# Feed-forward quarters per step redistributed around the tail step of each head pair, input sums moved with them

## The chip, the cores and the metric

The kernel runs on one core of a Trainium2 chip. The core has five engines with in-order queues: TensorE (PE in the profile, with PEld for its weight loads), VectorE (DVE), ScalarE (ACT), GpSimd (POOL) and SyncE (SP, which issues nearly all transfers here), and 16 DMA engines. The metric is the device time of one execution in microseconds; smaller is better.

## The reference

```python
scores = scale * np.matmul(q, k.transpose(0, 1, 3, 2))        # q, k, v: (8, 8, 576, 64)
thresh = np.max(scores, axis=-1, keepdims=True) - tau
scores = np.where(scores >= thresh, scores, -1000000000.0)
attn = np.exp(scores - np.max(scores, axis=-1, keepdims=True))
attn = attn / (np.sum(attn, axis=-1, keepdims=True) + 1e-09)
x = np.matmul(attn, v)                                        # -> (8*576, 512)
h = x @ w_in                                                  # 512 -> 2048
g = np.where(h > 0.0, h, np.exp(np.minimum(h, 0.0)) - 1.0)
out = g @ w_out                                               # 2048 -> 512
```

Attention with a threshold under each row's maximum, for 8 sequences of 8 heads, and then a feed-forward block (FFN) with an ELU between its two products. All is float32.

## The kernel before, in words

**Attention.** Heads go in pairs: 32 pairs, four to a sequence. A pair has five steps: four blocks of 128 queries for both heads, and one tail step for the 64 queries left over of each head. From pair 9 (`JOINED`) the order in a pair is block 0, block 1, tail, block 2, block 3; the text calls these places 0 to 4, so the tail step is place 2. A step of two heads runs so: scores on TensorE (`scores`, L236), row maximum on VectorE (L276), bound on GpSimd (L280), exponential on ScalarE (L285, L287), threshold mask and row sum on VectorE (L296 to L303), division on GpSimd (L272). One step later VectorE turns the weights in squares of 32 (`turn_squares`, L380, L390), SyncE writes them out (L394, L406), and one step after that fetches them back turned (`fetch`, L414, L418). The value products of the pair before run inside the tail step, interleaved with the tail's scores (`tails_and_values`, L466, L471, L478); ScalarE copies their result out (`values_out`, L487, L492). Two PSUM buffers named `sc` (one per head) serve the scores, and in the tail step one of them holds the values instead.

**FFN.** Each product is done on halves with seven products in place of eight, so there are sums of inputs, of weights and of results. A group is 512 tokens of one sequence; group g has two rounds r. A round is four units of the first product (`first_product`, L1016), 28 quarters, and then a second product (`second_round`, L1171) of 14 products in two quarters each, 28 quarters again. A quarter is four matmuls as the profile counts them. Behind a unit, ScalarE copies partial results out (L1030, L1082, L1083), GpSimd adds (L1035), VectorE adds (L1038), and then the ELU runs: exponential on ScalarE (L1049, and minus one at L1054, or on GpSimd at L1063), minimum and maximum on VectorE (L1071). GpSimd then forms sums of the results for the second product (L1108). The second product's results are added up on VectorE (L1180, L1189, L1191) and GpSimd (L1184) and stored (L556). Sums of weights are kept in DRAM and reloaded (`sw` L871 for the first product, `t` L901 for the second). `sums_x` (L907 to L909) makes five sums of a group's inputs, two of them in place, on VectorE; they have to follow the last values of that sequence and precede most of the group's first quarters.

**Order.** From step 45 (`MIDDLE`, pair 9, place 0) to the end of attention the order is written by hand as an agenda with times: `on_pe(cost, f)` issues TensorE work and advances a planned clock, and `at(t, f)` puts the other engines' work at planned times. In each step the loop issues the fetch, `softmax(n)` (the attention step), then `ffn_quarters(QUARTERS[place])`, which takes that many quarters from a queue of first and second products in fixed order. `QUARTERS` sums to 28, so each pair takes one first or one second product: odd pairs the first, even pairs the second. `group(b - 1)` puts the next group's products on the queue at place 3 of the first pair of a sequence, where its input sums are issued as well. `exp` of a unit is put off to 4.4 us after the start of a step when it would fall in the step's early part, except for the last unit's first half; ELUs put off in this way run at the end of a later step (`run_elus`), or when the second product asks for them. After the loop, what is left on the queue is taken without attention beside it, and then the last two groups follow.

Of the kernel before, what the change touches and what calls it, by code (L numbers as in the profile page):

```python
# [19 lines left out]
def kernel(  # L20
# [24 lines left out]
    NPAIR = H // 2  # L45
# [329 lines left out]
    def turn_squares(pr, i):  # L375
        w = open_steps.pop((pr, i))["w"]
        x = late["x"].tile([P, NT, NCH, T], FP32, name="x", bufs=2)

        def turn_part(c0, src, nc_):
            nc.vector.transpose(x[:, :, c0 : c0 + nc_], src.rearrange("p (c g n) -> p g c n", c=nc_, n=T))  # L380

        if i < NC:
            turn_part(0, w[:, :MAIN], NC)
            turn_part(NC, w[:, MAIN : MAIN + P], 1)
            turn_part(NC + 1, w[:, MAIN + P :], NC)
        elif pr >= JOINED:
            turn_part(1, w[:, :MAIN], NC)
            tail = w[:, MAIN:S].rearrange("p (g n) -> p g n", n=T).unsqueeze(1).broadcast_to([P, 2, 2, T])
            for g in (0, 2):
                nc.vector.transpose(x[:, g : g + 2, :: NC + 1].rearrange("p g c n -> p c g n"), tail)  # L390
            there = turns[pr, i] = dram.tile([NT, T, NT, (NC + 1) * T], FP32, name="there")
            for p in range(NT):
                h = int(p < 2)
                nc.sync.dma_start(  # L394
                    there[:, :, (p + 2) % NT].rearrange("c k n -> k c n"),
                    x[p * T : (p + 1) * T, :, 1 - h : NC + 2 - h].rearrange("k c j n -> k c (j n)"),
                )
            return
        else:
            turn_part(0, w[:, :MAIN], NC)  # L400
            turn_part(NC + 1, w[:, :MAIN], NC)
            for h in range(2):
                nc.vector.transpose(x[:, 2 * h : 2 * h + 2, NC], w[:, MAIN:S].rearrange("p (g n) -> p g n", n=T))
        there = turns[pr, i] = dram.tile([NT, T, NT, NCH * T], FP32, name="there")
        for p in range(NT):
            nc.sync.dma_start(  # L406
                there[:, :, p].rearrange("c k n -> k c n"), x[p * T : (p + 1) * T].rearrange("k c j n -> k c (j n)")
            )

    def fetch(pr, i):  # L410
        back = turns.pop((pr, i)).rearrange("c k p n -> (c k) p n")
        wT, g0 = turned_tile(pr, i)
        if i < NC:
            nc.sync.dma_start(wT[:, g0 : g0 + NT].rearrange("p g c n -> p g (c n)"), back)  # L414
        elif pr >= JOINED:
            for h in range(2):
                g = h * (3 * NT - 2)
                nc.sync.dma_start(  # L418
                    wT[:, g : g + 2, h * NC : h * NC + NC + 1].rearrange("p g c n -> p g (c n)"),
                    back[:, 2 * h : 2 * h + 2],  # L420
                )
        else:
            nc.sync.dma_start(
                wT.rearrange("p (a b) c n -> p a b (c n)", b=2)[:, ::5],
                back.rearrange("k (a b) n -> k a b n", b=2),
            )
# [163 lines left out]
    JOINED = (2 * NPAIR + 1)  # L590
    steps = [(pr, i) for pr in range(NP) for i in ((0, 1, NC, 2, 3) if pr >= JOINED else range(NB))]
# [42 lines left out]
    with tc.manual_schedule():  # L634
# [20 lines left out]
        for n in range(per_seq):  # L655
            pr, i = steps[n]
            hs = heads_of(i)
            x = progress[1]
# [86 lines left out]
    with tc.manual_schedule():  # L745
# [3 lines left out]
        for n in range(per_seq, SWITCH):  # L749
            pr, i = step = steps[n]  # L750
# [152 lines left out]
    def sums_x(g, rooms):  # L903
        (b11, b12), (b21, b22) = ([xts[g][:, k : k + 2, t : t + CT] for t in (0, CT)] for k in (0, 2))
        xs = in_sums["x", g] = rooms
        tt = nc.vector.tensor_tensor
        return [lambda: tt(xs[0], b11, b22, ALU.add), lambda: tt(xs[1], b11, b12, ALU.add),  # L907
                lambda: tt(b12, b12, b22, ALU.subtract), lambda: tt(xs[2], b21, b22, ALU.add),
                lambda: tt(b21, b21, b11, ALU.subtract)]  # L909
# [6 lines left out]
    with tc.manual_schedule():  # L916
        after = []
        make_out(1), make_out(0)
        for n in range(SWITCH, MIDDLE):
            pr, i = steps[n]  # L920
# [15 lines left out]
            else:  # L936
                if n == MIDDLE - 2:
                    jobs = sums_x(1, [late["x"].tile([P, 2, CT], FP32, name=f"x{x}") for x in range(3)])
# [26 lines left out]
        agenda, clock, now, serial = [], [0.0], [0.0], [0]  # L965

        def at(t, f):
            serial[0] += 1
            heapq.heappush(agenda, (t, serial[0], f))
# [9 lines left out]
        def on_pe(cost, f):  # L979
            until(clock[0])  # L980
            f()
            clock[0] += cost
            return clock[0]
# [245 lines left out]
        def group(g):  # L1229
            for r in range(2):  # L1230
                for u in range(RU * r, RU * r + RU):
                    queue.append((first_product, (g, u)))
                queue.append((second_round, (g, r)))
# [3 lines left out]
        def ffn_quarters(n):  # L1237
            while n and (quarters or queue):
                if not quarters:
                    f, a = queue.popleft()  # L1240
                    running[0] = f
                    mine = f(*a)

                    if (f, a) == (second_round, (B, 1)):
                        mine = [mine[x] for x in (0, 2, 6, 1, 3, 4, 5)] + mine[7:]
                    quarters.extend(mine)
                p, posts = quarters.popleft()
                end = on_pe(QT, p)
                for lag, f in posts:
                    at(end + lag, f)  # L1250
                n -= 1
# [45 lines left out]
        def values_of(pr, i):  # L1297
            if i in (1, NB - 1) and pr < JOINED:
                loc = {}
                part = 0 if i == 1 else 1  # L1300
                end = on_pe(3.1 if part else 2.3, lambda: loc.update(out=values(pr, part)))
                at(end + 0.1, lambda: loc["out"]())
# [6 lines left out]
            for out_ in outs:  # L1309
                out_()  # L1310

        QUARTERS = (7, 6, 2, 7, 6)
        group(1)
        for n in range(MIDDLE, len(steps) + 3):
            pr, place = divmod(n, NB)
            if n <= len(steps) + 1:
                at(clock[0] + (3.4 if place == 2 else 1.5), lambda n=n: fetch(*steps[n - 2]))
            if 0 < n - MIDDLE < 4:
                x = n - MIDDLE - 1
                at(clock[0] + 5.0, lambda x=x: nc.sync.dma_start(wout_sums[0, x], out_sums[x].rearrange("p u n -> p (u n)")))  # L1320
            if n == MIDDLE + NB:
                ges.append((raw.tile([P, S // T, T], FP32, name="km").rearrange("p j d -> p (j d)")[:, : 2 * CT], lambda: None))
            if n == len(steps):
                at(clock[0] + 2.0, lambda: turn_squares(*steps[-1]))
            if n < len(steps):
                softmax(n)
            b = pr // NPAIR
            if n < len(steps) and pr % NPAIR == 0 and place == 3 and b > 1:
                xs = [late["x"].tile([P, 2, CT], FP32, name=f"x{x}") for x in range(3)]
                jobs = sums_x(b - 1, xs)  # L1330
                for x, f in enumerate(jobs):
                    at(clock[0] + 4.2 + 0.5 * x + (4.0 if x > 2 else 0), f)
                group(b - 1)
            if n == len(steps) + 2:
                on_pe(5.0, last_values)
            ffn_quarters(QUARTERS[place])
            values_of(*steps[n - 3])
        attending[0] = False
        xs = [late["x"].tile([P, 2, CT], FP32, name=f"x{x}") for x in range(3)]
# [43 lines left out]
        xs = [qkp.tile([P, S], FP32, name="qT") for _ in range(2)] + [qkp.tile([P, TAIL + S], FP32, name="kT")]  # L1383
        xs = [x[:, : 2 * CT].rearrange("p (k t) -> p k t", k=2) for x in xs]
# [47 lines left out]
```

## Time and profile before

| | us |
|---|---|
| median of 6 runs | 1429.79 |
| lowest and highest run | 1426.63, 1439.89 |
| profiled execution, its own time | 1435.87 |
| its span, first to last instruction | 1434.0 |
| TensorE busy in the span | 1356.0 |
| VectorE, GpSimd, ScalarE busy | 1064.8, 817.1, 640.2 |
| mean granted TensorE clock | 0.985 |

The profile's page gives each engine's busy time and its share of the span; the views by line give, for a group of instructions, busy time, mean duration and the idle time of the engine just ahead of them with what ended it. In a timeline a row is a run of like instructions: start and length in us, engine, line, operation, output and inputs, shape, count, and in brackets the idle time before it and who ended it. The loop that the change touches runs from about 310 to 1234 us of the span; before it the attention of the first sequences runs with the weights' conversion, and after it only FFN work is left.

### The profile page before, as it was taken

How to read it: one execution, taken by the hardware profiler on the slowest of the kernel's cores; microseconds unless marked ns; L12 is line 12 of the kernel's file. 1: busy time of each engine (PE TensorE's matmuls, PEld its weight loads, DVE VectorE, ACT ScalarE, POOL GpSimd, SP SyncE). 2: the span in 40 equal slices, each digit the busy share in tenths (PEclk: the TensorE clock that was granted, in tenths of full speed). 3: DMA queues.
4: the chain of work that ended last, by engine and by line, in shares of the span. 5: the costliest groups of instructions: out<-in, count | busy, mean ns of one | idle time of the engine just before them, and what ended most of it. 6: DMA issues, size and time to landing. Idle time of an engine off the chain costs nothing.

```text
span 1434.0 us, 22711 instructions
## 1 busy us (share of the span) xinstructions
PE 1356.0 (95%) x6980; PEld 1006.9 (70%) x6980; DVE 1064.8 (74%) x2325; ACT 640.2 (45%) x1418; POOL 817.1 (57%) x1274
## 2 busy tenths in 40 slices
PE   9989999999999999998999999989999998999998
PEld 7656646556767677676767776767767676888887
DVE  6879995988778778887788778877787775546433
ACT  5776764235453536353444535353535443223311
POOL 4656774787466555656475647555564645425423
PEclk9998999999999999999999999999999999999999
DMA  5345433889878878686969787887879674421311
GB/s 111 73 108 144 132 101 77 252 245 256 222 199 225 219 186 239 174 241 174 239 168 272 171 230 200 237 215 178 235 175 252 165 224 124 137 66 46 117 55 30
DMA packets 322599, 247.80 MB, mean 173 GB/s; under 512 B 208688, under 2 KB 284464, under 8 KB 322480
## 3 DMA queue, kind: packets, MB, share of 16 engines
q1 hardware_dynamic: 320112, 246.07, 64.7%
q8 instruction: 56, 0.92, 0.3%
q10 hardware_dynamic: 2368, 0.30, 0.2%
q14 instruction: 63, 0.52, 0.1%
HBM read 161.81 MB, written 84.48 MB: 172 GB/s over the span
## 4 chain that ended last, share of the span: by engine, by line
PE 63%; DVE 14%; DMA 8%; POOL 6%; issue 4%; ACT 3%; SPq 2%; DVEq 0%; ACTq 0%; POOLq 0%
PE f L1171 20%; PE f L1016 16%; PE sc L236 8%; PE pv L478 6%; DVE mx L276 3%; PE rt L306 3%; DMA wTb<-there 3%; DMA there<-x 3%; DVE x L380 2%; PE f L527 2%; PE pv L440 2%; POOL s L1108 2%; PE f L567 2%; DVE w L296 2%; DVE g L1071 2%
## 5 line engine op out<-in xcount | busy, mean ns | idle before, releaser
L272 POOL TENSOR_SCALAR w<-w,rs 128x576 f32<-128x576 f32 x288 | 241.0, 841 | 152.4 <-DVE rs L303 135.5
L276 DVE TENSOR_REDUCE mx<-sc 128x1 f32<-128x576 f32 x270 | 193.0, 752 | 107.9 <-PE sc L236 82.6
L296 DVE SCALAR_TENSOR_TENSOR w<-sc,th,e 128x576 f32<-128x576 f32 x270 | 215.2, 813 | 34.1 <-ACT e L287 13.9
L287 ACT ACTIVATE e<-sc,nb,keep 128x576 f32<-128x576 f32 x270 | 223.2, 832 | 9.1 <-POOL nb L673 0.7
L285 ACT ACTIVATE nb<-mx,nkeep 128x1 f32<-128x1 f32 x254 | 74.7, 294 | 306.2 <-DVE mx L276 306.1
L236 PE MATMUL sc<-kT,qT 64*128 64x288 f32 x1024 | 175.7, 431 | 9.1 <-DVE w L296 7.8
L380 DVE STREAM_TRANSPOSE x<-w 128x512 f32<-128x512 f32 (+1 forms) x327 | 167.5, 560 | 0.0
L280 POOL TENSOR_SCALAR th<-mx,ntau 128x1 f32<-128x1 f32 x270 | 82.4, 306 | 146.7 <-DVE mx L276 145.4
L1171 PE MATMUL f<-w_out_sb,g 128*128 128x256 f32 x448 | 117.1, 396 | 40.6 <-DVE g L1071 40.6
L236 PEld LDWEIGHTS sc<-kT,qT 64*128 64x128 f32 x1024 | 99.2, 187 | 69.9 <-issue 48.8
L1016 PE MATMUL f<-xt,sw 128*128 128x256 f32 x512 | 130.1, 389 | 0.3 <-DVE g L1038 0.3
L1171 PEld LDWEIGHTS f<-w_out_sb,g 128*128 128x128 f32 x448 | 83.9, 194 | 65.1 <-DVE g L1071 50.6
L1016 PE MATMUL f<-xt,w_in_sb 128*128 128x256 f32 x512 | 121.1, 379 | 0.5 <-ACT w L1030 0.5
L1171 PE MATMUL f<-t,s 128*128 128x256 f32 x448 | 113.5, 387 | 1.4 <-DVE s L1108 0.7
L1016 PEld LDWEIGHTS f<-xt,sw 128*128 128x128 f32 x512 | 93.2, 190 | 29.9 <-issue 17.7
L1016 PE MATMUL f<-x,w_in_sb 128*128 128x256 f32 x448 | 109.0, 382 | 0.0
L1171 PE MATMUL f<-w_out_sb,s 128*128 128x256 f32 x448 | 108.8, 382 | 0.0
L1016 PEld LDWEIGHTS f<-xt,w_in_sb 128*128 128x128 f32 x512 | 97.2, 190 | 14.0 <-ACT w L1030 0.9
L1171 PEld LDWEIGHTS f<-t,s 128*128 128x128 f32 x448 | 82.1, 190 | 26.6 <-issue 8.2
L1016 PEld LDWEIGHTS f<-x,w_in_sb 128*128 128x128 f32 x448 | 84.1, 190 | 16.8 <-issue 5.4
L1035 POOL TENSOR_TENSOR u<-u,w 128x256 f32<-128x256 f32 x64 | 46.9, 733 | 85.1 <-ACT u L1030 85.1
L1171 PEld LDWEIGHTS f<-w_out_sb,s 128*128 128x128 f32 x448 | 84.2, 190 | 15.2 <-issue 4.2
(176 smaller groups left out, 2475.2 us busy)
## 6 DMA issues: line engine op xcount, KB each, us to landing
there<-x SPq DMA_DIRECT2D x408, 144.0 KB, 2.8
wTb<-there SPq DMA_DIRECT2D x52, 576.0 KB, 4.8
wTa<-there SPq DMA_DIRECT2D x50, 576.0 KB, 4.6
sw<-win_sums SPq DMA_DIRECT2D x62, 384.0 KB, 4.3
t<-wout_sums SPq DMA_DIRECT2D x45, 512.0 KB, 5.1
qm<-in_q_dram SPq DMA_DIRECT2D x128, 72.0 KB, 4.8
vm<-in_v_dram SPq DMA_DIRECT2D x64, 128.0 KB, 4.1
wst<-in_moe_w_in_dram SPq DMA_DIRECT2D x16, 512.0 KB, 4.6
```

Of the source, the lines that this page charges most:

```text
L236: nc.tensor.matmul(scs[h][:, a, :HALF], qs[r], kT[r, k0 : k0 + HALF], start=True, stop=True)
L272: nc.gpsimd.tensor_scalar(wv, wv, st["rs"][:, h : h + 1], 1.0, ALU.mult, ALU.mult)
L276: nc.vector.tensor_reduce(st["mx"][:, h : h + 1], st[h][:, :, :HALF], axis=AX.XY, op=ALU.max)
L280: nc.gpsimd.tensor_scalar(st["th"][:, h : h + 1], st["mx"][:, h : h + 1], 1.0, ntau, ALU.mult, ALU.add)
L285: nc.scalar.mul(st["nb"][:, h : h + 1], st["mx"][:, h : h + 1], nkeep)
L287: nc.scalar.activation(e, st[h][:, :, :HALF], AF.Exp, bias=st["nb"][:, h : h + 1], scale=keep)
L296: nc.vector.scalar_tensor_tensor(wv, sc[:, :, :HALF], st["th"][:, h : h + 1], e, ALU.is_ge, ALU.mult, accum_out=st["sm"][:, h : h + 1])
L380: nc.vector.transpose(x[:, :, c0 : c0 + nc_], src.rearrange("p (c g n) -> p g c n", c=nc_, n=T))
L478: nc.tensor.matmul(pv[h * D : (h + 1) * D, part, g0 * T : g1 * T], vm[:, h, c], parts[part][:, g0:g1, h * (NC + 1) + c], start=False, stop ...
L1016: nc.tensor.matmul(loc["banks"][place], left[:, j], right[:, j], start=(begins and j == 0), stop=(j == 1), skip_group_check=True)
L1035: nc.gpsimd.tensor_tensor(loc[name], x(), loc[other], op)
L1171: nc.tensor.matmul(place(m), lhs, rhs, start=(begins and v == 0), stop=(v == RU - 1), skip_group_check=True)
```

## The change

The five quotas of a pair keep their sum of 28 but are 7, 7, 2, 6, 6 instead of 7, 6, 2, 7, 6. Pair 9 has quotas of its own, 14, 14, 0, 6, 6, so that the queue runs 12 quarters ahead of the pairs from then on: a pair's quarters at places 3 and 4 belong to the product that the next pair ends at its place 2. In odd pairs the two quarters of place 2 are issued ahead of the tail's attention step instead of behind it. The input sums of a group, and the queueing of the group, move from place 3 to place 2, with other planned times.

```diff
-        QUARTERS = (7, 6, 2, 7, 6)
+        QUARTERS = (7, 7, 2, 6, 6)
+        BEGIN = (14, 14, 0, 6, 6)
         group(1)
         for n in range(MIDDLE, len(steps) + 3):
             pr, place = divmod(n, NB)
...
             if n == len(steps):
                 at(clock[0] + 2.0, lambda: turn_squares(*steps[-1]))
+            quota, ahead = (QUARTERS if pr > JOINED else BEGIN)[place], 0
+            if place == 2 and pr % 2:
+                ahead = quota
+                ffn_quarters(ahead)
             if n < len(steps):
                 softmax(n)
             b = pr // NPAIR
-            if n < len(steps) and pr % NPAIR == 0 and place == 3 and b > 1:
+            if n < len(steps) and pr % NPAIR == 0 and place == 2 and b > 1:
                 xs = [late["x"].tile([P, 2, CT], FP32, name=f"x{x}") for x in range(3)]
-                jobs = sums_x(b - 1, xs)
-                for x, f in enumerate(jobs):
-                    at(clock[0] + 4.2 + 0.5 * x + (4.0 if x > 2 else 0), f)
+                for x, f in enumerate(sums_x(b - 1, xs)):
+                    at(clock[0] + 0.4 + 0.7 * x, f)
                 group(b - 1)
             if n == len(steps) + 2:
                 on_pe(5.0, last_values)
-            ffn_quarters(QUARTERS[place])
+            ffn_quarters(quota - ahead)
             values_of(*steps[n - 3])
```

## The prediction

> **What bounds the kernel now.** I read the page first, then TensorE's waits between 320 and 1260 us (the hand-ordered loop), then its timeline at a few changes from first to second product, and last the other engines at the same moments.
>
> ```profile
> PE 1356.0 (95%) x6980; PEld 1006.9 (70%) x6980; DVE 1064.8 (74%) x2325; ACT 640.2 (45%) x1418; POOL 817.1 (57%) x1274
> ```
> ```profile
> PE f L1171 <- DVE g L1071: 40.6, 25, 4.3
> PE pv L471 <- DMA wTb<-there: 10.0, 8, 1.8
> PE sc L236 <- DVE w L296: 1.8, 5, 0.4
> ```
> TensorE is busy 95% of the span, and the loop's idle time has almost one name: the second product (L1171) waits 40.6 us in 25 places for the ELU on VectorE (L1071). Next come 10.0 us (plus one wait of 1.0 us without a named releaser) in which the tail step's value products (L471) wait for a turned weight block. So TensorE sets the end, and a wait removed from it counts in full unless another takes its place. Now one change, and the next:
>
> ```profile
> 497.75 1.24 PE L236 MATMUL sc<-kT,qT 64*128 64x288 f32 x8
> 498.92 1.56 PE L1171 MATMUL f<-w_out_sb,g 128*128 128x256 f32 x6
> 502.85 0.70 PE L1171 MATMUL f<-w_out_sb,g 128*128 128x256 f32 x2 [2.37 <-DVE g L1071]
> 503.39 1.89 PE L1171 MATMUL f<-t,g 128*128 128x256 f32 x8
> ...
> 577.49 1.17 PE L1171 MATMUL f<-w_out_sb,g 128*128 128x256 f32 x2 [2.38 <-DVE g L1071]
> 578.45 3.15 PE L1171 MATMUL f<-t,g 128*128 128x256 f32 x8
> ```
> The first product ends at 497.75. Between it and the first use of its last unit stand one set of scores (1.2 us) and six matmuls; the unit is ready at 502.8, some 5.0 us after the end (POOL's L1035 to 500.08, VectorE's sum 500.12, ScalarE's exponential and minus one 500.63 to 501.92, the ELU 502.12 to 502.80). The second change has the same wait, but afterwards eight matmuls take 3.15 us instead of 1.89. The columns of the next view are stretch, its length, five engines' busy time, then the granted clock and DMA:
>
> ```profile
> 499.00:508.00 9.00, 6.63 (x30) 5.27 (x32) 7.96 (x18) 4.56 (x9) 7.74 (x11) 1.00 0.60 171
> 574.00:583.00 9.00, 6.62 (x24) 5.20 (x23) 6.31 (x15) 4.20 (x8) 6.66 (x11) 0.81 0.58 167
> ```
> A granted clock of 0.81 over 9 us is 9 x 0.19 / 0.5 = 3.4 us at half speed, which costs 1.7 us and counts as busy time. Of the twelve changes' stretches eight read 0.81.
>
> **Part by part.** Work on TensorE is unchanged: a pair still has 28 quarters of about 0.89 us (L1016 x28 takes 6.24 us for 7). What moves is the order.
>
> *The change falls on the tail step.* In odd pairs the last two quarters of the first product go ahead of the tail's scores and values; then follow the tail (5.2 us at 515.42 to 520.58, where it waits for nothing) and a set of scores (1.2). The last unit is used about 1.5 us later, 7.9 us after the end against 5.0 needed. In the built order the last unit's first ELU stands ahead of the tail's maximum on VectorE, so nothing long is queued before it. I take all 25 waits as gone: **-40.6** (bounds -40.6 and -16; the latter leaves 1.0 us at each of 24 places).
>
> *The half-speed stretches* follow those waits, so I take the eight as gone: **-13.6** (8 x 1.7; bounds -13.6 and 0). Waits of 1.0 to 1.8 us at L471 were followed by none. The Trainium skill, "TensorE: Matmul & The Clock Gate", section "The HAM clock gate", says the clock drops after an idle window of about 3.4 us. Seven of the eight stretches here follow idle times of about 2.4 us or less, so by the rule they should not exist and nothing would be gained, and the forecast would stand 13.6 us higher; the rows decide.
>
> *The waits for the weight block move from odd to even pairs.* The block of a pair's last step is turned in the next pair's place 0, written out and fetched in place 1:
>
> ```profile
> 463.82 2.23 SPq L406 DMA_DIRECT2D there<-x  x4
> ...
> 471.08 0.96 SPq L414 DMA_DIRECT2D wTb<-there  x1
> ```
> ```profile
> 476.37 0.45 PE L471 MATMUL pv<-wTb,vd 64*64 64x320 f32 x1 [1.59 <-DMA wTb<-there]
> ```
> Place 0 began at 459.08, so the block came 17.2 us after it; over the odd pairs the trace's landings lie 14.1 to 17.3 us after, mean 15.9. The tail wants it 0.6 us after its own start. Odd pairs will have 7 + 7 + 2 quarters and two sets of scores ahead of the tail (16 x 0.89 + 2.4 = 16.6, wanted at 17.2): their 11.0 us go, **-11.0** (bounds -11 and 0). Even pairs have 14 quarters (14.9, wanted at 15.5) and lose the 3.2 us of idle time that covers them now; late ELUs no longer delay their place 0, so their block should come as the odd pairs' does. That is 0 to 1.8 us, 1.0 on average, in 11 even pairs: **+11** (bounds 0 and +20). SyncE's queue grows at that point: up to two output stores and the reload of an out-sum (L901) pass from the odd pair's place 0 into the even pair's places 0 and 1, ahead of the fetch; I lean to the pairs that have such traffic now (landing near 17 us).
>
> *A new wait: scores behind the tail.* The two quarters now stand between the tail's values and the scores of place 3. In odd pairs they go ahead of the tail, so this cover is gone. The scores of the second head need the score bank that holds the tail's values, which ScalarE must first copy out:
>
> ```profile
> 481.59 0.37 ACT L487 COPY xt<-pv 128x256 f32<-128x256 f32 x1 [2.46 <-PE pv L478]
> 481.86 0.63 ACT L1049 ACTIVATE ge<-g 128x512 f32<-128x512 f32 x1
> 482.53 0.63 ACT L1054 ACTIVATE ge<-ge 128x512 f32<-128x512 f32 x1
> 483.06 0.35 ACT L487 COPY xt<-pv 128x256 f32<-128x256 f32 x1
> 483.32 0.42 ACT L492 COPY xs<-pv 64x64 f32<-64x64 f32 x2
> ```
> ```profile
> 483.40 1.63 PE L236 MATMUL sc<-kT,qT 64*128 64x288 f32 x8
> ```
> The values end at 481.54, the copies at 483.74. Even behind two quarters the scores take 1.63 instead of 1.24 us: 0.39 is paid now. In the changed order one of the two exponentials (0.63) stays between the copies, so the bank is free 1.6 us after the values' end, and 0.3 of that passes in the first head's matmuls: a wait of 1.3, net +0.9 in 11 pairs: **+10** (bounds -4, if the copies come early, and +20, if both exponentials stand there). Behind it on TensorE everything queues.
>
> *Two steps of six quarters in succession* (places 3 and 4). From the scores' end VectorE runs maximum 1.42, turning 1.49, masks 1.64: with the scores 5.9 us, against 6.5 for the step. Two sums of 0.42 (L1180) can stand before the last mask in place 4. I put **+2** for 11 such places, and the old 1.8 go, **-1.8** (bounds 0 and +10). The Trainium skill, "SBUF — State Buffer", section "Who interferes with whom", speaks against the change here: a VectorE instruction with two SBUF inputs is blocked by a GpSimd instruction that reads SBUF, and the ELUs move beside GpSimd's sums. L1071 does take 0.67 to 1.21 us, but 0.5 us more stays inside the 2.9 us of slack.
>
> *Sums of inputs* (five of 0.68 us on VectorE, six groups) go from a step with two heads to the tail, which has one, and where place 3 begins about 1.9 us after the values. The first result wanted is the third quarter's; they end about at place 3's maximum. I cost it at nothing; without that cover it is 0.7 x 6 = 4.
>
> *Ends.* Pair 9 takes 14 quarters in each of places 0 and 1; its tail is short, so its next scores may wait for a mask: +1.5 (0 to 3). All 672 quarters now fit into the loop, so the 13 that follow it today no longer cover the last group's input sums (L907 to L909, 3.3 us on VectorE): product five would wait about 0.5; I put +1 (0 to 4).
>
> Sum: -40.6 - 13.6 - 11.0 - 1.8 + 11 + 10 + 2 + 1.5 + 1 = -41.5. The profiled execution took 1435.87 us (span 1434.0, 1.9 around it); 1435.87 - 41.5 = 1394.4. The runs before have a median of 1429.79 and spread over 13 us, as much as eight half-speed stretches cost, so I expect the changed kernel's runs near this floor and do not take off the 6 us between the two: **1394 us**.
>
> **Rivals.**
> - *The half clock stays.* The new waits of 1.3 to 1.8 us trip it as the 2.4 us ones do. For it: one wait of 1.91 us at 734 us did. Against: none at L471 did. 1394 + 13.6 = 1408.
> - *Transfers set the tails.* DMA engines are busy 80% of this loop, and a shorter loop has the same bytes: 0.80 x 77 / 73 = 84%. If each of 22 tails waits 1.8: 1394 - 11 + 40 = 1423.
> - *The covers hold better.* Blocks land in time and the bank is free early: 1394 - 11 - 10 = 1373.
> - *Slower: VectorE's chain sets the six-quarter steps.* 46 steps in places 3 and 4. With 41 us to eat, it decides from 0.9 us a step, that is a chain of 7.4 instead of 5.9 us with a reserve of 0.6. At 1.5 us: 1394 + 69 = 1463. For it: VectorE is busy 80% here, and sums now stand between masks. Against: today's six-quarter steps wait 0.4 us at most.
> - *The wait only moves*: the ELU comes late behind the tail too, 1.5 us at 12 changes (18): 1412.
>
> **How the numbers follow.** Forecast 0.60; half clock 0.10; transfers 0.07; better covers 0.10; wait moved 0.08; slower 0.05. Range 1376 to 1415: it reaches to the half clock, the moved wait and most of the better covers, and leaves out the last transfers and the slower case. About 0.5% (7 us) is what a measurement of this kernel can tell from no change. Faster by more than that: 0.91; within: 0.03; slower: 0.06.
>
> **What would show it.** Right: L1171's wait for L1071 near nothing in TensorE's waits; a granted clock of 1.00 at the changes; L471's waits in even tails alone; a new wait of 1 to 2 us at L236 behind the odd tails, released by ScalarE's copies. Wrong: L1071 still releasing L1171 in places 3 and 4; L236 waiting over 1 us for L296 in steps of six quarters; windows with a clock of 0.81 behind the new waits; waits over 2 us for the block.

## The result, and the profile after

The changed kernel takes 1429.14 us (median of 36 runs, 1419.41 to 1433.45), the kernel before beside it 1432.37 (76 runs): a ratio of 0.9975, 95% interval 0.9964 to 0.9986, 0.25% faster. The forecast was 1394, its range 1376 to 1415. The profiled execution took 1431.03 us with a span of 1429.2, against 1435.87 and 1434.0 before: 4.8 us less where 41.5 were expected.

The first line of the page of the changed kernel, and three groups of instructions further down (busy time and mean, then the idle time just ahead of them with its releaser):

```profile
PE 1353.2 (95%) x6980; PEld 1004.1 (70%) x6980; DVE 1056.5 (74%) x2319; ACT 642.9 (45%) x1418; POOL 818.6 (57%) x1280
...
L236 PE MATMUL sc<-kT,qT 64*128 64x288 f32 x1024 | 173.4, 440 | 34.8 <-DVE w L296 32.7
...
L1016 PE MATMUL f<-xt,sw 128*128 128x256 f32 x512 | 128.7, 387 | 12.5 <-DVE g L1038 12.5
...
L1171 PE MATMUL f<-w_out_sb,g 128*128 128x256 f32 x448 | 118.3, 411 | 0.0
```

The change did what it says: the second product (L1171) no longer waits for the ELU anywhere. But other lines now carry the idle time. TensorE's waits of the changed kernel between 310 and 1260 us (total, places, longest):

```profile
PE sc L236 <- DVE w L296: 26.6, 12, 2.4
PE f L1016 <- DVE g L1038: 12.5, 23, 1.7
PE pv L471 <- DMA wTb<-there: 6.4, 5, 2.2
PE pv L471 <- issue: 3.4, 4, 1.7
```

All waits of the loop add up to 51.6 us, against 55.2 before. The largest is new: scores (L236) waiting for a mask (L296), 2.34 us behind the tail of each of 11 odd pairs, and once 0.8 us in pair 9. TensorE's timeline at the first of these changes:

```profile
494.97 2.32 PE L478 MATMUL pv<-wTb,vm 128*64 128x320 f32 x16
499.63 1.33 PE L236 MATMUL sc<-kT,qT 64*128 64x288 f32 x8 [2.34 <-DVE w L296]
500.89 3.68 PE L1171 MATMUL f<-w_out_sb,g 128*128 128x256 f32 x8
504.41 1.89 PE L1171 MATMUL f<-t,g 128*128 128x256 f32 x8
```

The value products end at 497.3; place 3's scores need the score bank that the tail's mask still reads, and start at 499.6. The eight matmuls behind take 3.68 us where the next eight take 1.89. So the half-speed stretch is there again, behind the new wait. The windows over the same stretches as in the prediction say the same (the last three numbers are the granted clock, the DMA share and GB/s):

```profile
499.00:508.00 9.00, 8.37 (x34) 6.62 (x34) 6.74 (x19) 3.19 (x9) 5.13 (x9) 0.81 0.84 183
574.00:583.00 9.00, 6.72 (x19) 5.16 (x20) 6.84 (x16) 3.87 (x11) 6.68 (x12) 0.62 0.72 161
```

Why the mask is late is on VectorE's timeline of the changed kernel, at the same tail:

```profile
493.91 0.42 DVE L1038 TENSOR_TENSOR g<-f,t 128x256 f32<-128x256 f32 x1 [3.36 <-POOL t L1035]
494.25 0.41 DVE L1038 TENSOR_TENSOR g<-f,s 128x256 f32<-128x256 f32 x1
495.76 0.69 DVE L1071 SCALAR_TENSOR_TENSOR g<-km,g 128x512 f32<-128x512 f32 x1 [1.09 <-ACT km L1054]
496.37 0.75 DVE L276 TENSOR_REDUCE mx<-sc 128x1 f32<-128x576 f32 x1
497.03 1.49 DVE L380 STREAM_TRANSPOSE x<-w 128x512 f32<-128x512 f32 x3
498.66 0.82 DVE L296 SCALAR_TENSOR_TENSOR w<-sc,th,e 128x576 f32<-128x576 f32 x1
```

Read it as a queue. The tail's scores were there at about 493 (the tail began at 492.06), but its maximum (L276) stands in the queue behind the last unit's two sums and its first ELU. The sums wait 3.36 us for GpSimd, whose chain ends at 493.88; the ELU waits another 1.09 for ScalarE's minus one. Only then come maximum, turning and mask, and at 499.5 the bank is free. From 493 to 496.4 VectorE works on the last unit and waits for it, with the maximum ready in the queue behind. The code does this because the agenda hands out what is planned up to the value products before the tail pushes its own softmax items: the ELU, planned later than the maximum, still goes out ahead of it.

### The profile page after: what moved, and what is told of

Read it like the earlier page. It is cut to its first block, busy times and chain, and to the rows that moved or that the text cites. A ratio compares the mean times of both kernels' runs of the same rounds, so it can differ in the third digit from the quotient of the medians.

```text
span 1429.2 us, 22722 instructions
## 1 busy us (share of the span) xinstructions
PE 1353.2 (95%) x6980; PEld 1004.1 (70%) x6980; DVE 1056.5 (74%) x2319; ACT 642.9 (45%) x1418; POOL 818.6 (57%) x1280
## 4 chain that ended last, share of the span: by engine, by line
PE 70%; DVE 12%; POOL 5%; DMA 4%; ACT 4%; issue 3%; SPq 1%; DVEq 0%; ACTq 0%; POOLq 0%
PE f L1171 24%; PE f L1016 21%; PE sc L236 11%; PE pv L478 3%; DVE x L380 3%; PE rt L306 3%; PE f L527 2%; PE f L567 2%; DVE mx L276 2%; DMA wTb<-there 2%; PE pv L440 2%; POOL w L272 2%; DVE w L296 2%; ACT e L287 1%; DVE g L1038 1%
## 5 line engine op out<-in xcount | busy, mean ns | idle before, releaser
L276 DVE TENSOR_REDUCE mx<-sc 128x1 f32<-128x576 f32 x270 | 192.9, 751 | 71.4 <-PE sc L236 62.4
L296 DVE SCALAR_TENSOR_TENSOR w<-sc,th,e 128x576 f32<-128x576 f32 x270 | 213.9, 812 | 27.4 <-ACT e L287 11.6
L236 PE MATMUL sc<-kT,qT 64*128 64x288 f32 x1024 | 173.4, 440 | 34.8 <-DVE w L296 32.7
L280 POOL TENSOR_SCALAR th<-mx,ntau 128x1 f32<-128x1 f32 x270 | 78.8, 294 | 153.9 <-DVE mx L276 153.2
L236 PEld LDWEIGHTS sc<-kT,qT 64*128 64x128 f32 x1024 | 97.7, 190 | 94.3 <-issue 72.4
L1016 PE MATMUL f<-xt,sw 128*128 128x256 f32 x512 | 128.7, 387 | 12.5 <-DVE g L1038 12.5
L1016 PE MATMUL f<-xt,w_in_sb 128*128 128x256 f32 x512 | 121.8, 380 | 1.2 <-DVE xt L909 1.2
L1016 PEld LDWEIGHTS f<-xt,sw 128*128 128x128 f32 x512 | 94.2, 190 | 38.5 <-DVE g L1038 22.2
L1171 PE MATMUL f<-w_out_sb,g 128*128 128x256 f32 x448 | 118.3, 411 | 0.0
L1035 POOL TENSOR_TENSOR u<-u,w 128x256 f32<-128x256 f32 x64 | 57.4, 896 | 103.7 <-ACT u L1030 103.4
L1016 PE MATMUL f<-x,w_in_sb 128*128 128x256 f32 x448 | 111.3, 387 | 1.2 <-ACT g L1082 1.2
L1171 PE MATMUL f<-w_out_sb,s 128*128 128x256 f32 x448 | 110.0, 384 | 0.0
L1171 PE MATMUL f<-t,s 128*128 128x256 f32 x448 | 109.4, 387 | 0.4 <-POOL s L1108 0.3
L1016 PEld LDWEIGHTS f<-xt,w_in_sb 128*128 128x128 f32 x512 | 96.7, 190 | 16.6 <-ACT w L1030 1.9
L1171 PEld LDWEIGHTS f<-w_out_sb,g 128*128 128x128 f32 x448 | 91.8, 208 | 20.8 <-issue 7.1
L1016 PEld LDWEIGHTS f<-x,w_in_sb 128*128 128x128 f32 x448 | 82.3, 190 | 24.1 <-issue 8.5
L1171 PEld LDWEIGHTS f<-t,s 128*128 128x128 f32 x448 | 82.1, 190 | 23.8 <-issue 8.5
L1171 PEld LDWEIGHTS f<-w_out_sb,s 128*128 128x128 f32 x448 | 83.2, 190 | 20.5 <-issue 10.1
```

The costliest lines, as they stand in the source:

```text
L236: nc.tensor.matmul(scs[h][:, a, :HALF], qs[r], kT[r, k0 : k0 + HALF], start=True, stop=True)
L276: nc.vector.tensor_reduce(st["mx"][:, h : h + 1], st[h][:, :, :HALF], axis=AX.XY, op=ALU.max)
L280: nc.gpsimd.tensor_scalar(st["th"][:, h : h + 1], st["mx"][:, h : h + 1], 1.0, ntau, ALU.mult, ALU.add)
L296: nc.vector.scalar_tensor_tensor(wv, sc[:, :, :HALF], st["th"][:, h : h + 1], e, ALU.is_ge, ALU.mult, accum_out=st["sm"][:, h : h + 1])
L1016: nc.tensor.matmul(loc["banks"][place], left[:, j], right[:, j], start=(begins and j == 0), stop=(j == 1), skip_group_check=True)
L1035: nc.gpsimd.tensor_tensor(loc[name], x(), loc[other], op)
```

## The experiments

Each row's ratio is against runs of the kernel before on the same chip (its median in the last column). Chips differ by up to 5.7 us for the same kernel, so rows of different chips are compared by ratio: the changed kernel itself has 0.9975.

| run | edit | median us | ratio, 95% interval | before there |
|---|---|---|---|---|
| e1_elu_behind_max | last unit's ELU behind the tail's maximum, turning and mask | 1405.44 | 0.9818 [0.9793, 0.9842] | 1430.93 |
| e2_two_quarters_behind | no quarters ahead of the tail | 1411.96 | 0.9862 [0.9841, 0.9883] | 1430.93 |
| e3_sums_alone | kernel before, input sums moved alone | 1439.31 | 1.0053 [1.0035, 1.0072] | 1430.93 |
| e4_k_load_later | changed kernel, k load behind the fetch | 1417.49 | 0.9898 [0.9873, 0.9923] | 1430.93 |
| e5_elu_and_k_load | e1 and e4 | 1396.34 | 0.9743 [0.9718, 0.9767] | 1433.79 |
| e6_sums_behind_max_too | e5, last unit's sums behind maximum and turning too | 1395.23 | 0.9732 [0.9707, 0.9758] | 1433.79 |
| e7_sum_ahead_of_turn | e5, other units' first sum ahead of the turning | 1405.80 | 0.9806 [0.9780, 0.9832] | 1433.79 |
| e8_true_agenda | changed kernel, maximum alone ahead of the ELU | 1426.67 | 0.9947 [0.9924, 0.9969] | 1433.79 |
| e9_exp_behind_copies | e6, exponential behind ScalarE's copies | 1387.68 | 0.9720 [0.9694, 0.9745] | 1428.12 |
| e10_t_ahead_of_minus | e6, GpSimd's t ahead of its minus | 1394.33 | 0.9765 [0.9738, 0.9792] | 1428.12 |
| e11_both_orders | e9 and e10 | 1385.63 | 0.9708 [0.9681, 0.9736] | 1428.12 |
| e12_two_behind_and_k_load | e2 and e4 | 1401.15 | 0.9805 [0.9781, 0.9829] | 1428.12 |
| e13_t_and_sum_first | e11, sum ahead of the turning too | 1394.12 | 0.9721 [0.9693, 0.9749] | 1432.57 |

### e1: is it the order on VectorE?

```diff
+            last = attending[0] and v == RU - 1
...
-                [(0.6, lambda: add(h(0, 0), 2, "t5")), (1.3, lambda: exp(0))],
-                [(0.1, lambda: add(h(1, 1), 0, "s1")), (1.4 if attending[0] else 1.1, lambda: exp(1))],
+                [(2.15 if last else 0.6, lambda: add(h(0, 0), 2, "t5")), (3.3 if last else 1.3, lambda: exp(0))],
+                [(1.3 if last else 0.1, lambda: add(h(1, 1), 0, "s1")), (1.4 if attending[0] else 1.1, lambda: exp(1))],
```

> The changed kernel, with the last unit's exponential (and so its ELU) planned 2 us later in the odd pairs' tail steps, so that on VectorE the ELU stands behind the tail's maximum, turning and mask; its sums (L1038) stay ahead of the maximum. Theory (the gain was eaten by a new wait of 2.34 us of place 3's scores for the tail's mask, because the ELU stands ahead of the tail's maximum, and by the half-speed stretches behind it): the wait falls to 0.6 to 1.5 us, what stays being ScalarE's copies of the values; most clock readings of 0.5 behind the odd tails go; time 1400 to 1415. Rival 1 (the mask is late for another reason, GpSimd's queue or VectorE's load as a whole): the wait stays near 2.3 us and the time at 1425 to 1432. Rival 2 (the ELU is now late for the second product): L1171 waits for L1071 again, 1 to 2 us at 11 changes, time 1420 to 1430.

Measured: 1405.44, 24 us under the changed kernel's median (by ratio 22), with the same work and quotas. Its waits, and TensorE and VectorE at the same change (L1172 in this kernel is L1171 of before):

```profile
PE f L1016 <- DVE g L1038: 12.4, 23, 1.6
PE sc L236 <- DVE w L296: 7.5, 12, 1.5
PE sc L236 <- ACT xs L492: 3.3, 11, 0.3
```
```profile
492.18 0.72 PE L236 MATMUL sc<-kT,qT 64*128 64x288 f32 x2 [0.55 <-DVE w L296]
493.20 1.23 PE L236 MATMUL sc<-kT,qT 64*128 64x288 f32 x6 [0.30 <-ACT xs L492]
494.36 1.99 PE L1172 MATMUL f<-w_out_sb,g 128*128 128x256 f32 x8
```
```profile
488.24 0.42 DVE L1038 TENSOR_TENSOR g<-f,t 128x256 f32<-128x256 f32 x1 [3.35 <-POOL t L1035]
488.58 0.41 DVE L1038 TENSOR_TENSOR g<-f,s 128x256 f32<-128x256 f32 x1
488.91 0.75 DVE L276 TENSOR_REDUCE mx<-sc 128x1 f32<-128x576 f32 x1
489.57 1.49 DVE L380 STREAM_TRANSPOSE x<-w 128x512 f32<-128x512 f32 x3
491.20 0.82 DVE L296 SCALAR_TENSOR_TENSOR w<-sc,th,e 128x576 f32<-128x576 f32 x1
...
491.94 0.69 DVE L1071 SCALAR_TENSOR_TENSOR g<-km,g 128x512 f32<-128x512 f32 x1
```

Despite their later planned times the two sums still stand ahead of the maximum and wait 3.35 us for GpSimd; only the ELU has moved, behind the mask.

The mask's wait is 0.55 us in place of 2.34 (pair 9 apart), ScalarE's copies gate the second head as the prediction thought, and the eight matmuls take 1.99: no half speed. The mean granted clock rises from 0.984 to 0.9935. The second product still does not wait for the later ELU: the tail step gives it more cover than it needs. The ELU's place on VectorE is the cause of 1.8 of the 2.34 us.

### e2: are the two quarters ahead needed?

```diff
-                ahead = quota
-                ffn_quarters(ahead)
+                ahead = 0
```

> The changed kernel, with the two quarters of place 2 behind the tail in odd pairs too, as in even pairs. Theory (the quarters ahead of the tail take away the cover of place 3's scores, and in exchange cover the ELU): L236's wait of 2.34 us goes, L1171's wait for L1071 of about 2.4 us comes back, with its half-speed stretches: time within 6 us of the changed kernel's 1429. Rival (the place of these two quarters matters little, the tail step as such covers the ELU): both waits are small and the time is 1400 to 1415.

The rival was right: 1411.96, faster than the changed kernel by 17 us (by ratio 16). The change still falls on the tail step, but the last quarters come behind it. Its waits:

```profile
PE f L1171 <- DVE g L1071: 16.1, 22, 1.0
PE f L1016 <- DVE g L1038: 12.4, 23, 1.6
```

The ELU is late again, yet by 0.6 to 1.0 us and not 2.4, so nothing falls to half speed there (clock 0.994), and the new wait of the scores is gone (0.8 us in one place), because the ELU's chain starts behind the tail's mask. The change without the two quarters ahead would have brought more than with them.

### e3: the input sums alone

In the kernel before, only the sums and the queueing of the group move:

```diff
-            if n < len(steps) and pr % NPAIR == 0 and place == 3 and b > 1:
+            if n < len(steps) and pr % NPAIR == 0 and place == 2 and b > 1:
...
-                    at(clock[0] + 4.2 + 0.5 * x + (4.0 if x > 2 else 0), f)
+                    at(clock[0] + 0.4 + 0.7 * x, f)
```

> The kernel before, with only the input sums and the queueing of the group moved from place 3 to place 2 with the planned times of the change. Theory (the sums cost little either way): -1 to -6 us against before, from five waits of 0.35 us of the scores and the late steps around them. Rival (the sums carry what gain the change has, and the quotas alone are worth nothing or lose): -3 us or more, as much as the whole change.

Measured: slower, 1.0053, some 8 us, which neither side expected. In its profiled execution, one of its faster runs, L471's waits for the block are 14.2 us instead of 10.0 (longest 4.3, one place) and L1171 waits 2.2 us for a sum of results (L1189), 6.4 us more together. Over all runs half speed, counted as (1 - clock) x span, is 2.3 us more (medians of 23.7 and 21.4). That these make up the 8 us is likely, not shown, and why the blocks land later when sums move was not tried. Moving the sums has no gain of its own in the kernel before.

### e4: the k load in the even pairs

The next pair's k is loaded in place 0, on the queue that then writes and fetches the weight block. Here it goes behind the fetch:

```diff
-            if pr + 1 < NP and place == 0 and n > MIDDLE:
-                at(m + 0.9, lambda: load(pr + 1, ("km",), True))
+            if pr + 1 < NP and place == 1 and n > MIDDLE + 1:
+                at(t + 2.0, lambda: load(pr + 1, ("km",), True))
```

> The changed kernel, with the load of the next pair's k issued in place 1 behind the fetch instead of at the end of place 0 ahead of it on SyncE's queue. Theory (the even tails' waits for the weight block, 9.8 us in 9 places, come from SyncE's queue order and the traffic in front of the fetch): the waits fall to 0 to 5 us in all and the time by 3 to 8 us against the changed kernel. Rival (the block is late because its write to DRAM lands late, whatever stands ahead of the fetch): the waits stay within 2 us of 9.8 in all.

```profile
PE sc L236 <- DVE w L296: 26.6, 12, 2.4
PE f L1016 <- DVE g L1038: 12.5, 23, 1.7
PE pv L471 <- DMA wTb<-there: 2.5, 5, 0.8
```

Measured 1417.49, 11.7 us under the changed kernel (by ratio 11), more than expected. The even tails' waits go from 9.8 to 2.5 us (from the second even pair on their fetch is issued 8.1 to 9.7 us after the start of place 0, and 9.9 to 10.8 in the changed kernel), and the cost of half speed, counted as (1 - clock) x span, from 22.9 to 19.1 us: 7.3 + 3.8 = 11.1. The 26.6 us are untouched: two separate causes.

### e5 and e6: both together, and the ELU further back

e5 is e1 and e4 together. e6 puts the last unit's two sums behind the maximum and the turning too, ahead of the mask; its ELU stays behind the mask (planned lags 4.03, 3.18 and 4.07 instead of e1's 2.15, 1.3 and 3.3, one round excepted).

> The changed kernel with both edits of the first two that helped: the last unit's exponential and ELU behind the tail's maximum, turning and mask on VectorE, and the load of k behind the fetch on SyncE's queue. Theory (two separate causes): the gains add, 24 us and 11 us against the changed kernel's 1429, so 1390 to 1398, with L471's waits under 3 us and L236's under 12 in all. Rival (they share slack: without the 2.34 us waits the blocks are wanted earlier and the transfers set the tails): 1400 to 1406, L471's waits 6 us or more.

> As the kernel with both edits, and the last unit's two sums (L1038) stand behind the tail's maximum and turning too, from the second round on. Theory (what is left of the wait of place 3's scores is VectorE's sums waiting for GpSimd ahead of the maximum, 0.55 us, and ScalarE's copies of the values, 0.3): the 0.55 us go, the wait for ScalarE's copies grows to 0.8 to 1.3 us; the time falls by 0 to 4 us. Rival (the ELU then comes late for the second product): L1172 waits for L1071 by 0.5 us or more at each change and the time rises.

The gains add: e5 takes 1396.34, near the forecast. e6 clears the mask's wait behind the odd tails entirely (0.8 us are left, in pair 9), so the 0.55 us were the sums' wait for GpSimd; but then it waits 9.9 us in 11 places for ScalarE's copies, 0.90 each: the gate of which the prediction spoke. Its ScalarE at such a change:

```profile
494.32 0.37 ACT L487 COPY xt<-pv 128x256 f32<-128x256 f32 x1 [0.23 <-PE pv L478]
494.59 0.63 ACT L1049 ACTIVATE ge<-g 128x512 f32<-128x512 f32 x1
495.12 0.36 ACT L487 COPY xt<-pv 128x256 f32<-128x256 f32 x1
495.38 0.43 ACT L492 COPY xs<-pv 64x64 f32<-64x64 f32 x2
```

The exponential of the second half stands between the copies, as in the kernel before. In the changed kernel the mask was later still and hid this. e6's median is 1.1 us under e5's on the same chip, within their uncertainty.

### e8: was it the maximum alone?

The value parts' issue moves to the end of `softmax`, so that what is planned earlier goes out earlier: the maximum precedes the ELU, but the ELU still precedes turning and mask.

> The changed kernel, with the tail's attention work put on the agenda before the tail's value products are issued and not after, so that work planned up to 3.15 us into the tail no longer passes it on VectorE: the tail's maximum (planned at 1.2) then stands ahead of the ELU (planned at 1.83), which stays ahead of the turning and the mask. No other edit. Theory (the order of VectorE's queue in the odd tail is the cause of the 2.34 us wait): the wait falls by the part of the ELU's wait that the maximum no longer shares, to 0.9 to 2.0 us; time 1408 to 1425. Rival (only the sums' wait for GpSimd counts, and the ELU's place does not): the wait stays at 2.3 us, time 1426 to 1432.

The rival's numbers came, though not its reason, since in e1 the ELU's place does count: the wait falls from 2.34 to 2.18 us (24.7 in all) and the time hardly at all (1426.67). What the scores need is the mask, so the ELU has to stand behind that too. The profiled execution took 1414.86 at a clock of 0.992 where the median run had 0.9855; see the last section.

### e9, e10, e11: the two orders that are left

```diff
-                    at(begun[0] + 4.4, lambda: exp(c))
+                    at(begun[0] + (5.7 if end_unit else 4.4), lambda: exp(c))
...
-                    at(now[0] + (1.6 if c else 0.7), lambda: minus(c))
+                    at(now[0] + ((3.9 if attending[0] else 1.6) if c else 0.7), lambda: minus(c))
```

The first edit is e9's (`end_unit` is the `last` of e6), the second e10's; e11 has both.

> The kernel of e6 (last unit's sum and ELU behind all of the tail's softmax on VectorE, k load later), and in the step of an odd tail the second exponential (ScalarE, 0.63 us) is also moved behind the copies of the value products (place 3's scores wait 0.90 us for the last of these copies in 11 places of e6, 9.9 us in all). Theory: ScalarE's order alone sets that wait: the exponential stands 0.5 us of its 0.63 us between the copies, so the wait becomes 0.3 to 0.5 us, 3.3 to 5.5 us in all, and the time falls by 4 to 7 us, to 1388 to 1391. Rival: the copies wait for the value products on TensorE, or the exponential, now later, holds back the ELU whose values the second product needs: a new wait of the second product of 0.5 us or more takes the gain back, 1395 within 3.

> The kernel of e6, and in odd pairs GpSimd does the sum t of a unit ahead of the minus of the second exponential, not behind it (the minus took 1.05 us beside VectorE's ELUs). Theory: the 12.4 us that the first product waits for VectorE's sum (L1016 for L1038, 23 waits) are GpSimd's t, which stands behind that minus: the waits fall under 4 us and the time by 6 to 9 us, to 1386 to 1389. Rival: the bank is freed late because VectorE stands in its turning, and t is not what it waits for: the 12.4 us stay within 3 and so does the time; or the minus, now later, holds its ELU and the second product waits for it.

> The edits of e9 and e10 together on e6, the version that may beat both kernels. If both theories of those runs hold, their gains add as those of e1 and e4 did: 1380 to 1386. If either fails, the time is that of the other within 3 us; if the two edits get in each other's way (the ELU of the second exponential late on both counts), above the better of the two.

The exponential: the copies' wait falls from 9.9 to 4.2 us (0.38 in 11 places) as the theory said. What that is worth in time is less sure. On one chip, e11 against e10 is this edit alone: 1385.63 against 1394.33, 8.7 us less, more than the wait. But e9 against e6, the same edit on different chips, is 0.9720 against 0.9732: by ratio only 1.7 us, within the uncertainty, and short of the 4 to 7 expected. GpSimd's t: e11 against e9 is 2.1 us less, and e10 is no faster than e6 by ratio; the 12.4 us of L1016 became 11.2. So the rival held. e10's TensorE, and VectorE at the same moment:

```profile
474.48 1.13 PE L1016 MATMUL f<-xt,sw 128*128 128x256 f32 x4 [0.43 <-DVE g L1038]
```
```profile
473.44 0.67 DVE L380 STREAM_TRANSPOSE x<-w 128x512 f32<-128x512 f32 x1
474.04 0.39 DVE L1038 TENSOR_TENSOR g<-f,t 128x256 f32<-128x256 f32 x1
474.34 0.41 DVE L1038 TENSOR_TENSOR g<-f,s 128x256 f32<-128x256 f32 x1
```

The sum waits for nobody (no bracket): it follows the turning, and TensorE starts as it ends.

e11 is the fastest kernel of the study: 1385.63 us, 0.9708 of the kernel before (0.9681 to 0.9736), and by ratio 2.7% under the changed kernel (0.9708 / 0.9975). The 1380 to 1386 expected is met in time only: e6, from which it was counted, ran on a chip where the kernel before took 5.7 us longer. Its first line and its two largest waits in the loop:

```profile
PE 1335.1 (97%) x6980; PEld 992.6 (72%) x6980; DVE 1051.3 (76%) x2319; ACT 644.1 (47%) x1418; POOL 824.3 (60%) x1280
```
```profile
PE f L1016 <- DVE g L1038: 11.2, 23, 1.6
PE sc L236 <- ACT xs L492: 4.2, 11, 0.4
```

TensorE's busy time is 18 us less than in the changed kernel for the same 6980 instructions: matmuls at half speed count as busy.

### e7 and e13: the wait for the sum that frees a bank

e7 is e5 with product five's sum at a lag of 0.45 instead of 0.6, which puts it ahead of the turning; e13 is e11 with the same edit.

> As the kernel with both edits, and the other units' first sum (L1038) planned 0.15 us earlier, which puts it ahead of the turning (1.49 us) on VectorE where a unit ends two quarters into a step. Theory (the 12.4 us that L1016 waits for L1038 in 23 places are VectorE's order: the sum that frees the bank stands behind the turning, because the new quotas put the unit's end there): those waits fall under 5 us and the time by 3 to 8 us. Rival (GpSimd's part of the sum is what is late, at about the same moment): the waits stay, or come back at L236 as waits for L296, and the time does not fall.

> The kernel of e11 (all three orders mended) with the edit of e7 as well: in odd pairs VectorE's sum of a unit stands ahead of the turning, and GpSimd's part t stands ahead of the minus. Theory: the first product's 11 to 12.5 us of waits have two causes in a row, VectorE's turning in front of the sum and GpSimd's minus in front of t; e7 mended only the first and e10 only the second, and each left the other as the one that ends last. With both the waits of L1016 for L1038 fall from 11.2 us to under 3, and the time by 6 to 9 us from e11, to 1377 to 1380. Rival: GpSimd is late by its whole chain (the sums u and s stand ahead of t), not by the minus: the waits stay above 8 us, VectorE now waits in front of its turning, and the time stays at e11's 1386 within 3 or rises.

e7's rival was right: the waits grow to 19.4 us in 34 places, and the time rises by 9.5 us from e5. The first sum now stands in front of the turning and waits for GpSimd's t, so the second sum, behind the turning, comes later: in each odd pair two waits of 0.58 us are for the second sum and one of 0.45 for the first. With t earlier as well (e13) the wait stays, 11.7 us, but at another product, at both places of a pair for the second sum. e13's TensorE and VectorE:

```profile
481.63 1.13 PE L1016 MATMUL f<-x,sw 128*128 128x256 f32 x4 [0.29 <-DVE g L1038]
```
```profile
479.44 0.42 DVE L1038 TENSOR_TENSOR g<-f,t 128x256 f32<-128x256 f32 x1 [0.29 <-POOL t L1035]
479.78 1.49 DVE L380 STREAM_TRANSPOSE x<-w 128x512 f32<-128x512 f32 x3
481.19 0.38 DVE L1038 TENSOR_TENSOR g<-f,s 128x256 f32<-128x256 f32 x1
```

The first sum now frees its bank in time; the second (its output from `s`) stands behind the 1.49 us of turning, and the next product waits for that one. So my theory of two causes in a row fell: it is VectorE's turning, in front of whichever sum comes behind it. Both sums ahead of the turning, with t ready, was not tried. e13's time, 0.9721, is no better than e11's.

### e12: the quarters ahead, once more

> The kernel of e2 (first-product quarters all behind the scores, as in before, so that the ELU's place in the tail comes otherwise) with the later k load of e4. Theory: the two price different waits, so e4's gain over after (11.7 us) comes again on e2's 1412: 1400 within 3; the order on VectorE (e5, 1396) is then only slightly better than no quarters ahead. Rival: the gain of the k load in e4 was largely the half clock that a long tail wait set off; e2 has few such stretches, so only the waits themselves, some 6 us, come off: 1404 to 1408.

1401.15 us; scaled by ratio to e2's chip that is 1403, at the edge of the theory's 1400 within 3 and of the rival's 1404. The gain over e2 is 0.57%, some 8 us, and the waits of L471 fall by 7.1 (8.5 to 1.4), with the clock near 0.995 in both. So the gain is nearly that of the waits alone, as the rival had it; e4's extra was half speed, which e2 hardly has. Two quarters ahead are worth having only with the order on VectorE mended: on the same chip e10, with that order, lies 7 us under e12, and e9 and e11, with ScalarE's order mended too, 13 to 16 us.

## Why the prediction was wrong, point by point

By the profiled executions, term by term (us):

| term | predicted | measured |
|---|---|---|
| L1171's waits for L1071 | -40.6 | -40.6 |
| half speed in the loop | -13.6 | +5.1 |
| odd tails' blocks | -11.0 | -11.0 |
| even tails' blocks | +11 | +9.8 |
| scores behind odd tails, net | +10 | +21.5 |
| L1016's waits for L1038 | none | +12.2 |
| old L236 waits | -1.8 | -1.8 |
| six-quarter steps, pair 9, end | +4.5 | +2.0 |

The half speed is 11 stretches of 3.4 us in place of 8. The right column adds up to -2.8; early half-speed stretches, which vary by run, account for another -1.7, and the execution showed -4.8.

- **Right:** the second product's waits go in full; odd tails do not wait for their block and even ones wait 9.8 us in 9 places; steps of six quarters make no waits of their own, so the "VectorE's chain" rival was out; the last group's input sums make product five wait 1.2 us.
- **The step that failed** is the sentence "In the built order the last unit's first ELU stands ahead of the tail's maximum on VectorE, so nothing long is queued before it". The order was seen, and asked only what it means for the ELU. What stands *behind* the ELU was not asked: the tail's maximum, turning and mask, and through the bank place 3's scores. The 1.3 us was worked out from ScalarE's copies, which are done at 499.7 in the changed kernel too, but only because the exponential in front of them waits for that late maximum. The wait is 2.34 us, 25.8 in all behind 11 odd tails, net of the 0.39 x 11 = 4.3 that went: 21.5 for 10. Its releaser is VectorE's mask, not ScalarE's copies. e1 shows it: this order alone is worth 22 to 24 us, the half speed behind it included. The 1.3 us for the copies was the lesser error: with the mask out of the way (e6) they cost 0.90.
- **The half speed** followed from that. I had tied the stretches to the waits of 2.4 us, correctly, but the new waits are as long as the old. Gone waits and kept clock were two terms of one cause: with waits of 0.55 (e1) the clock is 0.9935, and 10 of the 13.6 us are there (two stretches are left in the loop, behind pair 9's tail and behind a wait of 3.1 us for a transfer); e5's profiled loop has none.
- **L1016's 12.5 us** had no term. The new quotas put the ends of units two quarters into a step, where VectorE is in its turning, so that the sum that frees the bank is 0.43 and 0.55 us late at two places of each odd pair. I had priced steps by VectorE's length of work, and not by where a unit ends in them.
- **Input sums** at nothing: alone they cost some 8 us in the kernel before (e3); what they cost in the changed kernel was not tried.
- Of the rivals, "the half clock stays" came true, though behind waits of 2.34 us and not of 1.3 to 1.8. "The wait only moves" came true in its words alone: the ELU is not late for the second product, and it is the scores that wait. Each was priced as if the rest of the forecast held; both together (1394 + 13.6 + 18 = 1426) come near the measured time, by luck.

With the ELU's order mended, e1 takes 1405.44, inside the forecast's range. That e5, with the k load moved as well, takes 1396.34, near the forecast's number, is partly luck: L1016's 12.4 us, which the forecast lacks, stand against blocks that wait 2.6 us where it had 11.

## What to carry to other kernels

When a chain of work is moved onto another step, list for each engine with an in-order queue not only what stands in front of the moved instructions but what now stands behind them, and who waits for that: an instruction that waits for two other engines holds up every ready one behind it. A planned time in an agenda is not the order in the queue; read the order as built, and move late work behind the softmax of its step before judging new quotas. Terms that share a cause, such as waits and the clock that follows them, stand or fall together and belong in one rival.

## What the runs showed of the hardware

- **A wait of 2 us can put TensorE at half speed, and where it falls in time decides.** Of the waits of 2.3 to 2.4 us at the changes, 6 of 9 were followed by a stretch of half speed before and 9 of 11 after; of e8's eleven of 2.18 us, 2 were. Shorter ones can do it too: one of 1.91 us did in the kernel before, and one each of 1.79 (e10), 1.74 (e8) and 1.46 us (e1). A stretch lasts 3.41 us, or twice that, at a granted clock of one half, and pairs that have one are 1.5 to 1.7 us longer (38.9 us from an odd place 0 to the next even one, 40.5 with one, 42.0 with two). The Trainium skill, "TensorE: Matmul & The Clock Gate", section "The HAM clock gate", speaks of an idle window of about 3.4 us; here shorter ones do it, though not each time.
- **The stretches begin on a fixed grid.** In the changed kernel's clock records they begin at 422.46, 500.97 and 576.06 us and so on: 78.51 and 75.09 us apart, 23 and 22 times 3.413. In each of the fifteen traces all stretches begin on one such grid. Count TensorE's longest idle piece within each slot of 3.41 us: over the loops of all traces, all 33 slots with 2.03 us or more were followed by half speed, 6 of 22 with 1.7 to 2.0, 1 of 28 with 1.4 to 1.7, and none of 3938 with less. The changed kernel's wait of 2.34 us at 652.83 is cut by a slot's end after 1.74 us and was followed by none. So the same wait costs 1.7 us more or not by where it falls on the grid; e8's profiled execution, 12 us under its median and some 9 of them by the clock, fits that. What decides between 1.4 and 2.0 us was not settled.
- **The spread of a kernel's runs is mostly this.** Span x clock, the time without half speed, is 1407 to 1411 us by chip for before and 1404 for after, and (1 - clock) x span is 20 to 23 us for both; within these kernels a run's span rises by 0.9 to 1.0 us for each us of the latter. e11 has 6 us of it, and its runs lie within 8 us.
